# Moving four weight conversions and two splits behind the split of x, at the end of a first layer

## The chip, the cores and the metric

The kernel runs on one core of a Trainium2 chip. The metric is the device time of one launch in microseconds (us). Before the change three runs gave 817.26, 816.15 and 817.18 us, a median of 817.18 us.

Five engines take part, each with its own list of instructions that it works through strictly in the written order: PE (TensorE, matmuls), DVE (VectorE), ACT (ScalarE), POOL (GpSimd) and SP (SyncE, which here only issues DMA transfers). They wait for each other by semaphores.

## The reference

Clustered attention for 2 batches of 8 heads (768 positions, head size 64), then two feed-forward parts on the 1536 x 512 result x:

```
attn = softmax(where(same cluster, q @ k.T / 8, -1e9)) @ v     # per batch and head
a = x @ w1 ;  b = x @ w2                                        # 512 -> 1024  (the first layer)
h = ((a * b) @ w3) @ w_out                                      # 1024 -> 1024 -> 512
g = h2 @ w_in ; g = max(g, 0) + alpha * min(g, 0) ; g @ w_out2  # 512 -> 2048 -> 512
```

The weights arrive as 64-bit floats, all else is 32-bit; products are formed from a high and a low part of each factor.

## The kernel before, in words

**High and low parts.** Each factor of a matmul is held as two tiles in a reduced 32-bit format, a high part (a cast) and a low part (the difference). `mm3` (L243 to L246) forms one product with three matmuls: high x high, high x low, low x high.

**Weights.** They arrive as 64-bit words. For one tile of 128 x 512 weights the kernel does a *conversion* in two halves (`w_step`, L190): the first half loads the raw words of the conversion three places later (`w_load`, L132, a DMA on SP into one of **four** raw buffers `wr`), unpacks on ACT (L176, into `wu`) and joins the bits on DVE with three instructions (L181, L182, L185, into `wt`, two buffers). The second half casts on ACT (L226) and subtracts on POOL (L227). L182 is the last reader of a raw buffer on DVE, so a load on SP into a raw buffer waits for L182 of the conversion four places earlier.

**Reloads.** The high and low parts of the first layer's weights are stored to DRAM (`kept`, L148) when batch 0 uses them and are loaded again for batch 1 (L200, tile `wh`, one of five buffers). Batch 0 and batch 1 both go through the first layer in blocks of 128 outputs; a block takes two weight tiles, one for w1 (`l1a`) and one for w2 (`l1b`).

**One list sets the order of weights.** `seq` (L71 to L118) holds, in order: the first layer's 16 conversions (numbers 0 to 15), the conversions of four tiles of w_out (16 to 19, tiles `wo0`, `wo1`), the reloads of block 0 for batch 1 (20 and 21), two more conversions of w_out (22 and 23), the reloads of block 1 (24 and 25), two conversions (26 and 27), and so on. Numbers in names of tiles such as `wt17`, `wr22` and `wh20` are places in this list. `w_goal(n)` (L232) advances it by one half of a conversion if it has not passed n; `w_ready(key)` (L239) advances it until the wanted weights are there. Nothing in the list overtakes anything else, and what the list asks of SP is issued by SP in that order.

**The end of batch 0's first layer.** The attention loop (L729) interleaves attention with blocks 0 to 5 of the first layer of batch 0. Behind the loop, L807 runs what is left: blocks 6 and 7, in eight steps of 12 matmuls (l1a and l1b for each half of 384 positions, `a` = 0 and 1). After each step it calls `w_goal` up to conversion 23 (L808) and, while there is something ready, splits one finished product tile into high and low (`p_split`, L793: casts L799 on ACT, subtractions L800 on DVE, into `ph` and `pl`). The products themselves are `pr` (L594 on DVE, reading the PSUM result of l1b and a copy `asb` of l1a that ACT makes in L590).

**The split of x.** Then `x_split(1, p, a)` (L565) makes the high and low part of x for batch 1: eight casts on ACT (L570), four subtractions on DVE for a = 0 and four on POOL for a = 1 (L572), all into `xs`. `xs` for batch 1 lies in the buffer that `xs` for batch 0 held, so the first cast waits for the last matmul of batch 0's first layer. Behind it come the splits of products still open, then the first layer of batch 1 (L820), whose first matmul reads `wh20` and `xs`.

Of the kernel before, what the change touches and what calls it, by code (L numbers as in the profile page):

```python
# [28 lines left out]
def kernel(  # L29
# [41 lines left out]
    seq, at, keep, need = [], {}, {}, {}  # L71
# [118 lines left out]
    def w_step(force=False):  # L190

        n = st["step"]
        if n == NSEQ:
            return False
        kind, key, src = seq[n]
        if kind == "k":
            if not w_room():
                assert not force, key
                return False
            nc.sync.dma_start(out=f32(whl_tile(n)), in_=kept[src])  # L200
            st["step"] += 1
            return True
        m = ordinal[n]
        if not st["half"]:
            w_load(m + 3)
            while stores and ordinal[stores[0]] <= m - 2:
                w_store()
            w_u(m)
            w_conv(n)
            w_u(m + 1)  # L210
            st["half"] = 1
            return True
        if key[0] == "wo":
            if key[2] not in WO:
                return False
            hi, lo = WO[key[2]]
        else:
            if not w_room():
                assert not force, key
                return False  # L220
            t = whl_tile(n)
            hi, lo = his[key]
            if key[0] in ("l1", "w45", "e"):
                whole[n] = t
                stores.append(n)
        nc.scalar.copy(out=hi, in_=tts[n])  # L226
        nc.gpsimd.tensor_tensor(out=lo, in0=tts.pop(n), in1=f32(hi), op=ALU.subtract)  # L227
        st["half"] = 0
        st["step"] += 1
        return True  # L230

    def w_goal(n):  # L232

        while st["step"] <= min(n, NSEQ - 1):
            k = seq[st["step"]][0] == "k"
            if not w_step() or not k:
                return

    def w_ready(key):  # L239
        while st["step"] <= at[key]:  # L240
            w_step(True)
# [17 lines left out]
    def j_load(b, g, c):  # L259
        nc.sync.dma_start(out=j_raw(b, g)[:, c], in_=qka[b, g, c])  # L260
# [322 lines left out]
    def l1(b, f, a, alloc):  # L583

        if b not in PR:
            PR[b] = cp.tile([P, 8 * S], F32, tag="pr", name=f"pr{b}").rearrange("p (f s) -> p f s", f=8)
        t = alloc(f"l1a{b}{f}{a}")
        l1_mm(t[:, 0:HS], b, f, 0, a)
        q = wp.tile([P, HS], F32, tag="asb", name=f"asb{b}{f}{a}")
        nc.scalar.copy(out=q, in_=t[:, 0:HS])  # L590
        yield
        t = alloc(f"l1b{b}{f}{a}")
        l1_mm(t[:, 0:HS], b, f, 1, a)
        nc.vector.tensor_tensor(out=PR[b][:, f, a * HS : a * HS + HS], in0=t[:, 0:HS], in1=q, op=ALU.mult)  # L594
        yield


    with tc.manual_schedule():
# [45 lines left out]
        def l1_steps(b, f, ahead):  # L644
            for a in range(2):
                if a == 0:
                    w_ready(("l1", b, f, 1))
                for _ in l1(b, f, a, alloc_f):
                    w_goal(ahead)
                    yield f  # L650
# [10 lines left out]
        def fill_steps():  # L661

            yield from j01
            jm = cp.tile([P, 8 * S], F32, tag="wox", name="jm1")
            PR[0] = cp.tile([P, 8 * S], F32, tag="pr", name="pr0").rearrange("p (f s) -> p f s", f=8)
            sn = PR[0][:, 5:7].rearrange("p f s -> p (f s)")
            jmem[1, 0] = jm, jm[:, 3072 : 4608], jm[:, 5376 : 6144]
            jmem[1, 1] = jm, sn, PR[0][:, 7]
            for c in range(3):
                j_load(1, 0, c)  # L670
                yield
            j10, j11 = job(1, 0, alloc_f), job(1, 1, alloc_f)
            for k in range(5):
                next(j10)
                yield
            j_load(1, 1, 0)
            next(j10)
            yield
            for k in range(6):
                if k < 2:  # L680
                    j_load(1, 1, k + 1)
                next(j11)
                yield
            for _ in j10:
                yield
            for _ in j11:
                yield
            for _ in range(4):
                w_goal(1)
                yield  # L690
            while len(xdone) < 4:
                yield
            for f in range(8):
                yield from l1_steps(0, f, at["l1", 0, f, 0] + 3)


        cur = [alloc_s]
# [24 lines left out]

        xdone, fill_at = [], [0]
        fill = fill_steps()

        LT = 4
# [66 lines left out]
        def p_split(b, f, a):  # L793
            if (b, a) not in PH:
                for d, n in ((PH, "ph"), (PL, "pl")):
                    d[b, a] = big(f"{n}{a}", f"{n}{b}{a}").bitcast(F32R).rearrange("p (f s) -> p f s", f=8)
            s = slice(a * HS, a * HS + HS)
            ph, pl = PH[b, a][:, f], PL[b, a][:, f]
            nc.scalar.copy(out=ph, in_=PR[b][:, f, s])  # L799
            nc.vector.tensor_tensor(out=pl, in0=PR[b][:, f, s], in1=f32(ph), op=ALU.subtract)  # L800
# [4 lines left out]
        WO["wc"] = xp.tile([P, 2, 8, 512], F32R, tag="wc", name="wc")  # L805
        nsp = 0
        for f in fill:  # L807
            w_goal(at["wo", 0, 5, 0])  # L808
            if f is not None and nsp < f:
                p_split(0, nsp, 0), p_split(0, nsp, 1)  # L810
                nsp += 1
        for a in range(2):
# [140 lines left out]
```

## Time and profile before

| | us |
|---|---|
| median of three runs | 817.18 |
| the profiled execution | 814.83 |
| its span, first to last instruction | 812.7 |
| PE busy in the span | 760.2 (94%) |
| DVE busy | 525.1 (65%) |
| ACT busy | 452.1 (56%) |
| POOL busy | 303.1 (37%) |

The span is 2.13 us shorter than the profiled execution's own time. PE's 94% is an average: the attention stage (until about 334 us) has many short waits, and the stages behind it few. The rows below are of the stretch around 352 us, where batch 0's first layer ends and batch 1's begins.

### The profile page before, as it was taken

To read this page: it belongs to the slowest core of one execution; us is meant where nothing else is said; L and a number is where in the kernel's file an instruction comes from. 1 tells how busy PE (TensorE), PEld (TensorE's weight loads), DVE (VectorE), ACT (ScalarE), POOL (GpSimd) and SP (SyncE) were. 2 spreads that over 40 slices of the span, in tenths; PEclk is the share of its full clock that TensorE was granted. 3 is DMA by queue.
4 is the path that set the end of the run, shared out by engine and by line. 5 is a ranking of instruction groups with operands and counts; after the bars stand their busy time and mean duration, and the time that the engine had idled before them with its cause. 6 is when DMAs were issued, how large, how long until landed. Compare 5 with 4: busy or idle time off the path is not lost.

```text
span 812.7 us, 12622 instructions
## 1 busy us (share of the span) xinstructions
PE 760.2 (94%) x4497; PEld 699.8 (86%) x4497; DVE 525.1 (65%) x884; ACT 452.1 (56%) x980; POOL 303.1 (37%) x286
## 2 busy tenths in 40 slices
PE   5889899869999999969999999999999999999998
PEld 2678888769999998959999999998989878999996
DVE  3786899988888888885545599434456763322223
ACT  5799888877777787553223345324444453323232
POOL 0586778887676755433212343101112220000000
PEclk9899999999999999979999999999999999999999
DMA  7565343535464525755534588115665738333332
GB/s 243 179 173 159 85 97 83 133 93 162 130 179 127 165 77 157 233 181 181 181 130 158 173 276 289 64 40 194 192 204 182 219 135 280 122 121 127 128 130 78
DMA packets 38862, 127.27 MB, mean 157 GB/s; under 512 B 5168, under 2 KB 5296, under 8 KB 38800
## 3 DMA queue, kind: packets, MB, share of 16 engines
q1 hardware_dynamic: 38800, 126.46, 50.0%
q8 instruction: 36, 0.59, 0.3%
q14 instruction: 26, 0.21, 0.1%
HBM read 84.08 MB, written 28.31 MB: 138 GB/s over the span
## 4 chain that ended last, share of the span: by engine, by line
PE 65%; DVE 14%; ACT 5%; issue 4%; POOL 2%; DMA 1%; SPq 0%; POOLq 0%; ACTq 0%; DVEq 0%
PE l L246 7%; PE l L244 7%; PE l L245 7%; PE acc L245 5%; PE acc L246 5%; PE acc L244 5%; PE t L510 3%; DVE pl L520 3%; PE l1a L245 2%; PE l1a L244 2%; PE l1a L246 2%; PE l1b L245 2%; PE l1b L246 2%; PE l1b L244 2%; PE lc L245 2%
## 5 line engine op out<-in xcount | busy, mean ns | idle before, releaser
L227 POOL TENSOR_TENSOR wh<-wt,wh 128x512 fp32r<-128x512 f32 x64 | 86.3, 1348 | 232.2 <-ACT wh L226 160.3
L520 DVE TENSOR_TENSOR pl<-t,ph 128x384 fp32r<-128x384 f32 x192 | 97.5, 549 | 27.0 <-ACT ph L519 26.4
L867 DVE SCALAR_TENSOR_TENSOR gr<-gr,alp 128x384 f32<-128x384 f32 x64 | 41.6, 650 | 107.4 <-ACT gr L866 107.4
L510 PE MATMUL t<-cst,p 128*128 128x128 f32 x576 | 83.9, 282 | 22.3 <-DVE pl L520 22.2
L519 ACT CAST ph<-t 128x384 fp32r<-128x384 f32 x192 | 83.3, 484 | 30.1 <-PE t L510 28.6
L495 POOL TENSOR_SCALAR p<-p,su 128x768 f32<-128x768 f32 x96 | 91.9, 963 | 15.4 <-DVE su L492 13.2
L477 DVE TENSOR_REDUCE nm<-s 128x1 f32<-128x768 f32 x96 | 91.0, 948 | 3.2 <-PE s L470 3.2
L510 PEld LDWEIGHTS t<-cst,p 128*128 128x128 f32 x576 | 65.0, 143 | 30.9 <-issue 18.7
L484 ACT ACTIVATE p<-s,nm 128x768 f32<-128x768 f32 x96 | 88.2, 918 | 1.8 <-DVE nm L477 1.8
L469 PE MATMUL s<-st 128*128 128x384 f32 x192 | 75.1, 391 | 3.5 <-ACT p L484 3.5
L865 ACT ACTIVATE gr<-l 128x384 f32<-128x384 f32 x64 | 31.2, 487 | 80.6 <-PE l L246 80.6
L531 PE MATMUL o<-ph,vs 128*128 128x256 f32 x288 | 75.9, 291 | 0.0
L246 PE MATMUL acc<-wh,g 128*128 128x512 f32 x192 | 75.3, 392 | 0.0
L244 PE MATMUL acc<-wh,g 128*128 128x512 f32 x192 | 74.8, 390 | 0.6 <-ACT os L891 0.6
L245 PE MATMUL acc<-wh,g 128*128 128x512 f32 x192 | 75.3, 392 | 0.0
L532 PE MATMUL o<-pl,vs 128*128 128x256 f32 x288 | 73.8, 285 | 0.0
L182 DVE SCALAR_TENSOR_TENSOR wt<-wr,wt 128x512 uint32<-128x512 uint32 x72 | 70.5, 980 | 2.5
L470 PE MATMUL s<-st 80*128 80x384 f32 x192 | 67.5, 352 | 1.5 <-DMA st<-mk 1.5
L870 ACT CAST g<-gr 128x384 fp32r<-128x384 f32 x64 | 32.8, 513 | 59.5 <-DVE gr L867 59.5
L185 DVE SCALAR_TENSOR_TENSOR wt<-wu,wt 128x512 uint32<-128x512 uint32 x72 | 63.1, 876 | 2.5
L226 ACT CAST wh<-wt 128x512 fp32r<-128x512 f32 x64 | 39.8, 622 | 40.8 <-DVE wt L185 21.1
L544 POOL TENSOR_TENSOR xr<-xt 64x256 f32<-64x256 f32 x48 | 37.5, 782 | 64.6 <-ACT xt L543 57.7
(137 smaller groups left out, 1972.0 us busy)
## 6 DMA issues: line engine op xcount, KB each, us to landing
wh<-kept SPq DMA_DIRECT2D x58, 512.0 KB, 3.5
wr<-in_w_dram SPq DMA_DIRECT2D x48, 512.0 KB, 5.1
kept<-wh SPq DMA_DIRECT2D x48, 512.0 KB, 5.5
wr<-in_w3t_dram SPq DMA_DIRECT2D x16, 512.0 KB, 4.3
jm<-in_qka_dram SPq DMA_DIRECT2D x12, 512.0 KB, 5.6
hr<-in_qkh_dram SPq DMA_DIRECT2D x16, 384.0 KB, 3.4
st<-st SPq DMA_DIRECT2D x16, 384.0 KB, 3.7
st<-st SPq DMA_DIRECT2D x32, 192.0 KB, 2.7
```

What stands on the lines that cost most here:

```text
L227: nc.gpsimd.tensor_tensor(out=lo, in0=tts.pop(n), in1=f32(hi), op=ALU.subtract)
L244: nc.tensor.matmul(o, lhsT=whi, rhs=xhi, start=first, stop=False)
L245: nc.tensor.matmul(o, lhsT=whi, rhs=xlo, start=False, stop=False)
L246: nc.tensor.matmul(o, lhsT=wlo, rhs=xhi, start=False, stop=last)
L469: nc.tensor.matmul(t[:, a, 0:HS], lhsT=s[:, 0, q], rhs=s[:, 1, ks], start=True, stop=False)
L477: nc.vector.tensor_reduce(out=m, in_=scp[i][:, :, 0:HS], op=ALU.max, axis=AX.XY, negate=True)
L484: nc.scalar.activation(out=p.rearrange("p (a k) -> p a k", a=2), in_=scp.pop(i)[:, :, 0:HS], func=AF.Exp, bias=nmax.pop(i), scale=1.0, acc ...
L495: nc.gpsimd.tensor_scalar(out=pt[i], in0=pt[i], scalar1=sums[i // 2][:, i % 2 : i % 2 + 1], scalar2=1.0, op0=ALU.mult, op1=ALU.mult)
L510: nc.tensor.transpose(t[:, k], pt[i][:, kt * P : kt * P + P], ident)
L519: nc.scalar.copy(out=pth[g][:, 3 * a : 3 * a + 3, q], in_=t)
L520: nc.vector.tensor_tensor(out=ptl[g][:, 3 * a : 3 * a + 3, q], in0=t, in1=f32(pth[g][:, 3 * a : 3 * a + 3, q]), op=ALU.subtract)
L531: nc.tensor.matmul(ob[g], lhsT=w, rhs=pth[g][:, kt], start=(kt == 0), stop=False)
```

## The change

Three edits. In the attention loop's filler, block 7 no longer advances the weight list past its own weights (the number 3 becomes 0). In the loop over the remaining steps, the call that advanced the list by half a conversion per step is gone. And the splits of products inside that loop stop after six tiles, where they went on to seven.

```
@@ -691,7 +691,7 @@
             while len(xdone) < 4:
                 yield
             for f in range(8):
-                yield from l1_steps(0, f, at["l1", 0, f, 0] + 3)
+                yield from l1_steps(0, f, at["l1", 0, f, 0] + (3 if f < 7 else 0))
@@ -805,8 +805,7 @@
         WO["wc"] = xp.tile([P, 2, 8, 512], F32R, tag="wc", name="wc")
         nsp = 0
         for f in fill:
-            w_goal(at["wo", 0, 5, 0])
-            if f is not None and nsp < f:
+            if f is not None and nsp < min(f, 6):
                 p_split(0, nsp, 0), p_split(0, nsp, 1)
                 nsp += 1
```

What stands behind the loop is the same text in both kernels: the split of x, the splits of products still open (now tiles 6 and 7, before tile 7 alone), and the first layer of batch 1, which first calls `w_ready` for block 0's weights.

**DVE, blocks 6 and 7 of batch 0, before.** `pr0<-l1b060` is the product of block 6, half 0; `wt17` and `wt18` are conversions 17 and 18; `pl` are splits of products.

```order
L594 TENSOR_TENSOR pr0_506<-l1b060_4433,asb060_4421 128x384
L181 TENSOR_SCALAR wt17_4450<-wu17_4396 128x512
L182 SCALAR_TENSOR_TENSOR wt17_4450<-wr17_4305,wt17_4450 128x512
L185 SCALAR_TENSOR_TENSOR wt17_4450<-wu17_4396,wt17_4450 128x512
L800 TENSOR_TENSOR pl00_4426<-pr0_506,ph00_4425 128x384
L800 TENSOR_TENSOR pl01_4430<-pr0_506,ph01_4429 128x384
L800 TENSOR_TENSOR pl00_4426<-pr0_506,ph00_4425 128x384
L800 TENSOR_TENSOR pl01_4430<-pr0_506,ph01_4429 128x384
L594 TENSOR_TENSOR pr0_506<-l1b061_4468,asb061_4462 128x384
```

Behind these rows the product of block 6, half 1 is followed by conversion 18 in the same way, and so on: one conversion between two products.

**DVE, behind the last product of batch 0, now.** Ahead of these rows stand the product `pr0<-l1b071` and the first subtraction of the split of x; `xs1` is the split of x for batch 1, a = 0.

```order
L572 TENSOR_TENSOR xs1_4552<-xr5_2935,xs1_4552 128x384
L572 TENSOR_TENSOR xs1_4552<-xr6_3481,xs1_4552 128x384
L572 TENSOR_TENSOR xs1_4552<-xr7_3977,xs1_4552 128x384
L800 TENSOR_TENSOR pl00_4424<-pr0_506,ph00_4423 128x384
L800 TENSOR_TENSOR pl01_4428<-pr0_506,ph01_4427 128x384
L800 TENSOR_TENSOR pl00_4424<-pr0_506,ph00_4423 128x384
L800 TENSOR_TENSOR pl01_4428<-pr0_506,ph01_4427 128x384
L181 TENSOR_SCALAR wt17_4582<-wu17_4396 128x512
L182 SCALAR_TENSOR_TENSOR wt17_4582<-wr17_4305,wt17_4582 128x512
L185 SCALAR_TENSOR_TENSOR wt17_4582<-wu17_4396,wt17_4582 128x512
L181 TENSOR_SCALAR wt18_4592<-wu18_4586 128x512
L182 SCALAR_TENSOR_TENSOR wt18_4592<-wr18_4363,wt18_4592 128x512
```

Conversions 17, 18, 19 and 22 (twelve DVE instructions) moved from between the products to behind the split of x and the two last splits of products; 19 and 22 follow the rows shown, and then the first product of batch 1.

**SP, the loads and reloads around the same place, now; before, the same instructions stand in the same order.** `wr` are raw loads, `kept` a store, `wh20` and `wh21` the reloads that block 0 of batch 1 reads.

```order
L137 DMA wr22_4579<-in_wo_dram 128x1024
L148 DMA kept_73<-wh15_4386 128x1024
L137 DMA wr23_4590<-in_wo_dram 128x1024
L137 DMA wr26_4600<-in_wo_dram 128x1024
L200 DMA wh20_4610<-kept_73 128x1024
L200 DMA wh21_4612<-kept_73 128x1024
```

Nothing moved on SP; `wr23` goes into the raw buffer of conversion 17 and `wr26` into that of conversion 18. On POOL the subtractions (L227) of conversions 16 to 19 moved behind its four subtractions of the split of x, and on ACT their casts behind the eight casts of the split of x and the casts of the last two splits of products.

## Rows read from the trace of the kernel before

**Rows 1.** Waits of PE over the whole span: us in total, times, longest.
```profile
PE l1a L245 <- DVE xs L572: 4.0, 1, 4.0
PE l1a L244 <- DVE pl L800: 3.9, 1, 3.9
...
PE l L244 <- ACT gr L866: 1.2, 3, 0.5
```

**Rows 2.** Timeline of PE: start, length, instruction, [idle before <- releaser].
```profile
351.31 0.34 PE L246 MATMUL l1b<-xs,wh 128*128 128x384 f32 x1
355.57 0.69 PE L244 MATMUL l1a<-xs,wh 128*128 128x384 f32 x1 [3.93 <-DVE pl L800]
360.30 0.69 PE L245 MATMUL l1a<-xs,wh 128*128 128x384 f32 x1 [4.04 <-DVE xs L572]
360.78 0.52 PE L246 MATMUL l1a<-xs,wh 128*128 128x384 f32 x1
361.10 0.52 PE L244 MATMUL l1a<-xs,wh 128*128 128x384 f32 x1
...
364.36 0.34 PE L244 MATMUL l1b<-xs,wh 128*128 128x384 f32 x1
```

**Rows 3.** PE by stretch: us, PE busy (matmuls), granted clock, DMA share, GB/s.
```profile
352.00:356.00 4.00, 0.43 (x1) 0.73 0.57 198
356.00:360.00 4.00, 0.26 (x1) 0.50 0.34 112
360.00:364.00 4.00, 3.70 (x10) 0.50 0.74 282
364.00:368.00 4.00, 4.00 (x24) 0.99 0.00 0
```

**Rows 4.** Timeline of SP's queue and of ACT, 347 to 359 us.
```profile
347.20 0.33 SPq L137 DMA_DIRECT2D wr<-in_wo_dram  x1
347.58 0.90 SPq L200 DMA_DIRECT2D wh<-kept  x2
...
355.02 3.39 ACT L570 CAST xs<-xr 128x384 fp32r<-128x384 f32 x8
358.32 0.92 ACT L799 CAST ph<-pr 128x384 fp32r<-128x384 f32 x2
```

**Rows 5.** Timeline of DVE, 346 to 364 us.
```profile
346.43 0.69 DVE L182 SCALAR_TENSOR_TENSOR wt<-wr,wt 128x512 uint32<-128x512 uint32 x1
347.16 0.69 DVE L185 SCALAR_TENSOR_TENSOR wt<-wu,wt 128x512 uint32<-128x512 uint32 x1
347.77 1.02 DVE L800 TENSOR_TENSOR pl<-pr,ph 128x384 fp32r<-128x384 f32 x2
...
358.90 4.36 DVE L572 TENSOR_TENSOR xs<-xr,xs 128x384 fp32r<-128x384 f32 x4
```

**Rows 6.** Waits of SP's queue, 330 to 395 us; reloads in that stretch, issue to landing.
```profile
SPq L137 <- DVE wt L182: 47.3, 11, 9.4
...
DMA to landing us min/median/max: 3.1/4.9/6.0
```

**Rows 7.** Reloads issued 347.5 to 347.9 and 358.0 to 358.3 us: size, us to landing.
```profile
wh<-kept SPq DMA_DIRECT2D x1, 512.0 KB, 4.5
...
wh<-kept SPq DMA_DIRECT2D x1, 512.0 KB, 4.7
```

**Rows 8.** Timeline of POOL, 353 to 363 us.
```profile
353.81 1.34 POOL L227 TENSOR_TENSOR wo<-wt,wo 128x512 fp32r<-128x512 f32 x1 [3.87 <-ACT wo L226]
357.25 5.12 POOL L572 TENSOR_TENSOR xs<-xr,xs 128x384 fp32r<-128x384 f32 x4 [2.10 <-ACT xs L570]
```

**Rows 9.** DVE's L800, L181, L182: ns shortest/median/longest, 330 to 372 us.
```profile
L800 DVE TENSOR_TENSOR pl<-pr,ph x16: 545/551/1408, 338.6 to 363.6; 128x384 fp32r<-128x384 f32 x16
L181 DVE TENSOR_SCALAR wt<-wu x8: 409/414/774, 329.7 to 371.4; 128x512 uint32<-128x512 uint32 x8
L182 DVE SCALAR_TENSOR_TENSOR wt<-wr,wt x8: 691/693/1734, 330.1 to 371.8; 128x512 uint32<-128x512 uint32 x8
```

More of the change, by code (lines that the diff above doesn't have):

```diff
@@ L693, in fill_steps @@
             for f in range(8):
-                yield from l1_steps(0, f, at["l1", 0, f, 0] + 3)
+                yield from l1_steps(0, f, at["l1", 0, f, 0] + (3 if f < 7 else 0))
         cur = [alloc_s]
@@ L807 @@
         for f in fill:
-            w_goal(at["wo", 0, 5, 0])
-            if f is not None and nsp < f:
+            if f is not None and nsp < min(f, 6):
                 p_split(0, nsp, 0), p_split(0, nsp, 1)
```

## The prediction

> **What bounds the kernel now.** I read PE's waits first. Behind the attention stage PE has three waits in one place, the change from batch 0 to batch 1 in the first layer (4.0 and 3.9 us), and then next to none to the end of the span: the largest later line is 1.2 us in three waits [rows 1]. So from the first layer of batch 1 on, PE is the bound, and whatever delays or advances PE at this place moves the end by as much.
>
> The timeline of PE shows the place [rows 2]. The last matmul of batch 0 starts at 351.31 and ends at 351.65. The first of batch 1 starts at 355.57, the second at 360.30, and the next tile, l1b, at 364.36. The reader should see two things: two long holes, and matmuls 0.32 us apart (360.78 to 361.10), for which PE's granted clock was 0.50, that is 1.2 of 2.4 GHz, after it had stood nearly idle [rows 3]. The first 12 matmuls thus end 12.7 us after batch 0 did.
>
> What ended the two holes? The first matmul needs the reloaded weights `wh20` and the first cast of the split of x. `wh20` was issued at 347.58 and took 4.5 us, so it lay there at 352.1 [rows 4, 7]. ACT's casts of x began only at 355.02 [rows 4]; that ended the first hole (the row names a subtraction L800 on DVE, but the matmul follows the first cast by half a microsecond). The second hole ended with DVE's first subtraction of x, begun at 358.90 [rows 5]. DVE and ACT were late because a conversion stood between the products and the splits. The weights were early, and only just: 3 us.
>
> **The change part by part.**
>
> *What it takes away.* Conversions 17, 18, 19 and 22 leave DVE's, ACT's and POOL's lists ahead of the split of x, as does one split of products. DVE's part of one conversion is 0.41 + 0.69 + 0.69, 1.85 us from start to start of what follows [rows 5, 9]. Without them DVE follows PE: the last product starts at about 351.75 and ends at 352.3, since it waits for the last matmul (351.65). ACT's first cast of x waits for the same matmul, because the new tile lies in the old one's buffer: 351.7. So x's first high part would be there at 352.2 and its first low part at 352.9. By the split of x alone PE would start 3.4 us sooner and not wait a second time.
>
> *What it moves, and who stands behind it.* SP's list is unchanged, and in it the reloads `wh20` and `wh21` stand behind the raw loads `wr23` and `wr26`. A raw load waits for the L182 of the conversion whose buffer it takes; such waits are most of SP's waiting, 47.3 us in eleven [rows 6]. The traced load at 347.20 is `wr26`: it left 0.08 us behind the end of conversion 18's L182 (346.43 + 0.69), and `wh20` 0.38 us behind it [rows 4, 5]. The change puts conversion 18 behind the split of x and the last two splits of products on DVE. So `wh20`, which lay ready at 352.1, is now issued only when DVE has come through all that. This is the wait that takes the place of the one removed, and it is worked out along DVE:
>
> 1. Split of x. POOL's first subtraction followed ACT's first cast by 2.23 us (355.02 to 357.25) [rows 4, 8], so now POOL begins at 353.9. Until then DVE runs at the 0.5 us a piece that a pair takes alone (1.02 for two) [rows 5], three of its four subtractions; the fourth ends at 354.4.
> 2. Splits of tiles 6 and 7. ACT's eight casts take 3.39, until 355.1, and its next cast 0.5 [rows 4]: the first of four `pl` starts at 355.6. POOL is in its subtractions until 353.9 + 5.12 = 359.0 [rows 8]. Beside POOL, DVE's four subtractions of x took 4.36 us [rows 5]; alone two `pl` took 1.02. Bounds for the four: 2.0 alone and 4 x 1.408 = 5.6 at the longest seen [rows 9]. I take 4.4, the row with POOL in the same work: 360.0. (At the lower bound ACT's casts, two in 0.92, hold them to 357.5.)
> 3. Conversion 17: 1.85 alone; POOL's L227 of conversion 16, 1.34 long [rows 8], runs from 359.0 to 360.3, so I add 0.3 for the overlap: 362.15. Bounds 1.85, and 0.77 + 1.73 + 0.69 = 3.2 with the longest L181 and L182 [rows 9].
> 4. Conversion 18 up to L182: 0.42 + 0.69 and the gap, 1.15: 363.3. Upper bound 0.77 + 1.73 = 2.5.
> 5. SP: 0.08 + 0.38: `wh20` is issued at 363.75. Two reloads in the same neighbourhood, each right behind a raw load, landed after 4.5 and 4.7 us [rows 7]; all of the stretch lie between 3.1 and 6.0 [rows 6]. With 4.7: 368.45.
> 6. PE starts then, everything else being ready, on the lower clock as in the traced start [rows 3]: 12 matmuls at 0.32, 3.8 us, so l1b starts at 372.25. Bounds 2.0 (at full clock 24 matmuls fill a stretch of 4.0 [rows 3]) and 4.1, what eleven took before with waits in them.
>
> On the Trainium skill, SBUF — State Buffer, section "Who interferes with whom": a DVE operation with two operands in SBUF and a GpSimd operation that reads SBUF exclude each other, the second to come standing still until the first is done. Here the shortest `pl` is 545 ns and the longest 1408, which a lock with an operation of POOL in the way would give, so the trace does not speak against it [rows 9]. Applied to every `pl` and L182 beside POOL, it is the long case below.
>
> The Trainium skill, DMA: Bandwidth & Descriptors, section "Anatomy of one DMA", fits a transfer as 2.0 us plus its bytes at 436 GB/s (for descriptors made by software). For 512 KB this is an estimate of 3.2 us against the 4.5 and 4.7 measured; by it the sum would be 1.5 us smaller. The measurement stands.
>
> *The sum.* l1b starts at 372.25 instead of 364.36: 7.9 us later. The later conversions on DVE end at about 368, ahead of the first product of batch 1, and the reloads of block 1, behind conversion 22, have until 372.25 + 3 x 2.0 (12 matmuls at full clock), about 378.2; both lie beside PE's work. If that cover failed, it would show as a PE wait at block 1. Nothing later gives time back, since PE hardly waits later [rows 1]. The profiled execution, 814.83 with its span of 812.7, would become 822.7; it lay 2.35 below the median of the three runs, 817.18, and that becomes 825.1. I forecast 825.
>
> At the lower bounds together (357.5, then 1.85, 1.15, 0.46, a landing in 3.1, 2.0 on PE) l1b starts at 366.05, 1.7 us late: 818.9. At the upper bounds of the DVE steps (355.6 + 5.6 + 3.2 + 2.5 = 366.9), a landing in 6.0 and 4.1 on PE, 377.5: 13.1 us late, 830.3.
>
> **The rivals.**
>
> *Faster: the split of x decides alone.* If `wh20` is not held back (the raw load ahead of it gets its buffer at the old time), PE starts at 352.2, and l1b follows at 355 to 356.7 by the two spacings: 7.7 to 9.4 us gained, 807.8 to 809.5. For it: both holes of the trace are those of the split of x [rows 2]. Against it: SP issues in its written order, and the row at 347.20 leaves 0.08 us behind the very instruction that moves. It decides if `wh20` lands before 352.2.
>
> *No change.* Between the two: `wh20` lands about when PE now goes on, near 360.3 and less the 0.5 that the waits inside cost. That asks for conversion 18's L182 at about 355.5, when ACT has just ended its casts of x and two splits and a conversion still lie ahead. Only a DVE list other than the one shown would give it.
>
> *The lock everywhere.* Every `pl` takes 1.408, and L182 1.73 beside POOL's L227: four `pl` until 361.2, conversion 17 until 364.4, the next L182 at 366.5, `wh20` at 371.65 and l1b at 375.5, 11.1 us late, 828.3. The page of the skill named above would make this the rule. Against it: the four subtractions of x took 4.36 beside POOL, not 5.6 [rows 5], and POOL has only four of its own left to put in the way.
>
> **How the numbers follow.** The forecast (5 to 10 us slower) gets 0.76. The lock everywhere (over 10) gets 0.08. A smaller loss (1.7 to 5 us: short landing, DVE hardly hindered) gets 0.07. Faster gets 0.06, no change 0.03. A measurement of this kernel can tell 0.2%, 1.6 us, from no change. So slower is 0.91, within 0.2% is 0.03, faster 0.06. The range leaves out the faster and unchanged cases and the far ends of the slower ones: 821 to 829.
>
> **What would show it.** In the changed profile, ACT's casts of x begin near 351.7 and DVE's first subtraction of x near 352.3; that step is right even if the time is not. SP's wait for DVE's L182 at `wr26` ends near 363.4. PE has one hole of about 16.8 us instead of 3.9 and 4.0, ended by a DMA into `wh`, then 12 matmuls at clock 0.50. DVE's `pl` of the last two tiles are the widest term. I am wrong if PE's first matmul of batch 1 follows the cast of x by less than a microsecond, or if reloads are issued before 355.

## The result and the profile after

The changed kernel took 824.78 us (median of four runs, 822.12 to 825.47) against 816.66 for the kernel before (four runs, 816.03 to 817.26): a ratio of 1.0097, 95% interval 1.0074 to 1.0119, or 8.1 us slower. Forecast were 7.9 slower and 825. That the medians meet the forecast so closely is partly luck: the interval spans 6.0 to 9.7 us, and the stretch that the change touches grew by 9.3, as shown below.

The profiled executions differ by more, 825.47 to 814.83, and the reason has to be cleared away before anything is compared. In the profile after, batch 0's first layer ends at 353.40, in the one before at 351.65 [rows 2]. The change did not make that difference: the very first matmul of the first layer, far ahead of anything that moved, starts at 183.35 before and at 185.09 after, so 1.74 of the 1.75 us are there already. Over the twelve profiles of this study, one for each kernel, the end of batch 0's first layer lies between 350.51 and 356.14. From here on times are counted from that end, called E, in each profile. A second mark, the first matmul that joins w3 and w_out (tile `lc`), closes the stretch, three blocks later.

PE's longest waits in the profile after (us in total, times, longest):

```profile
PE t L510 <- DVE pl L520: 21.8, 21, 4.2
PE l1a L244 <- DMA wh<-kept: 17.6, 1, 17.6
...
PE l1a L244 <- DVE pr L594: 0.7, 1, 0.7
```

The two waits of before [rows 1] are gone; one wait of 17.6 for a reload stands there. Timeline of PE after, and then its granted clock by stretch (us, PE busy, clock, DMA share, GB/s):

```profile
353.06 0.34 PE L246 MATMUL l1b<-xs,wh 128*128 128x384 f32 x1
370.95 0.66 PE L244 MATMUL l1a<-xs,wh 128*128 128x384 f32 x1 [17.56 <-DMA wh<-kept]
371.41 0.52 PE L245 MATMUL l1a<-xs,wh 128*128 128x384 f32 x1
...
374.93 0.52 PE L244 MATMUL l1b<-xs,wh 128*128 128x384 f32 x1
...
377.48 0.33 PE L244 MATMUL l1a<-xs,wh 128*128 128x384 f32 x1
...
398.28 0.39 PE L244 MATMUL lc<-wo,wh 128*128 128x512 f32 x1
```

```profile
362.00:366.00 4.00, 0.00 (x0) 0.50 0.38 131
366.00:370.00 4.00, 0.00 (x0) 0.50 0.93 310
370.00:374.00 4.00, 3.04 (x10) 0.50 0.96 368
374.00:378.00 4.00, 4.00 (x20) 0.76 0.62 240
```

From E to `l1b` were 364.36 - 351.65 = 12.71 before and are 374.93 - 353.40 = 21.53 now, 8.8 more; the lower clock lasts three matmuls into `l1b`, and to `lc` it is 398.28 - 353.40 = 44.88 against 35.60 (before, `lc` starts at 387.25), 9.3 more. From `lc` to the end of the span it is 823.7 - 398.28 = 425.4 now and 812.7 - 387.25 = 425.4 before: nothing was given back and nothing lost later.

Timelines of DVE and of SP's queue after, 353 to 366 us:

```profile
353.50 0.56 DVE L594 TENSOR_TENSOR pr<-l1b,asb 128x384 f32<-128x384 f32 x1 [2.74 <-PE l1b L246]
353.98 1.96 DVE L572 TENSOR_TENSOR xs<-xr,xs 128x384 fp32r<-128x384 f32 x4
357.28 4.96 DVE L800 TENSOR_TENSOR pl<-pr,ph 128x384 fp32r<-128x384 f32 x4 [1.34 <-ACT ph L799]
362.16 0.41 DVE L181 TENSOR_SCALAR wt<-wu 128x512 uint32<-128x512 uint32 x1
...
364.40 0.69 DVE L182 SCALAR_TENSOR_TENSOR wt<-wr,wt 128x512 uint32<-128x512 uint32 x1
```

```profile
363.37 2.13 SPq L137 DMA_DIRECT2D wr<-in_wo_dram  x2
365.55 0.90 SPq L200 DMA_DIRECT2D wh<-kept  x2
```

This is the chain of the forecast, link by link: the split of x starts with the end of batch 0 (its four subtractions on DVE now take 1.96 us where they took 4.36 [rows 5]), then four `pl`, then conversion 17, then conversion 18's L182, which ends at 365.09; 0.08 later SP issues the raw load that stood ahead, and 0.46 later the reload. In the kernel before, the same reload was issued 4.1 us ahead of batch 0's end. SP's longest single wait for L182 was 24.6 us; it was 9.4 [rows 6].

### The profile page after: what moved, and what is told of

It is laid out like the page before. It is cut to its first block, busy times and chain, and to the rows that moved or that the text cites. A ratio compares the mean times of both kernels' runs of the same rounds, so it can differ in the third digit from the quotient of the medians.

```text
span 823.7 us, 12629 instructions
## 1 busy us (share of the span) xinstructions
PE 762.4 (93%) x4497; PEld 703.7 (85%) x4497; DVE 525.6 (64%) x884; ACT 451.9 (55%) x980; POOL 302.6 (37%) x286
## 4 chain that ended last, share of the span: by engine, by line
PE 67%; DVE 10%; ACT 6%; issue 4%; POOL 2%; DMA 1%; SPq 0%; POOLq 0%; ACTq 0%; DVEq 0%
PE l L246 7%; PE l L244 7%; PE l L245 7%; PE acc L245 5%; PE acc L246 5%; PE acc L244 5%; PE t L510 4%; PE l1a L244 3%; DVE pl L520 3%; PE l1a L246 3%; PE l1a L245 3%; PE l1b L244 2%; PE l1b L246 2%; PE l1b L245 2%; PE lc L245 2%
## 5 line engine op out<-in xcount | busy, mean ns | idle before, releaser
L227 POOL TENSOR_TENSOR wh<-wt,wh 128x512 fp32r<-128x512 f32 x64 | 86.2, 1347 | 231.7 <-ACT wh L226 145.0
L495 POOL TENSOR_SCALAR p<-p,su 128x768 f32<-128x768 f32 x96 | 91.6, 959 | 18.5 <-DVE su L492 16.4
L510 PEld LDWEIGHTS t<-cst,p 128*128 128x128 f32 x576 | 65.4, 144 | 30.6 <-issue 18.8
L182 DVE SCALAR_TENSOR_TENSOR wt<-wr,wt 128x512 uint32<-128x512 uint32 x72 | 70.5, 980 | 2.5
L185 DVE SCALAR_TENSOR_TENSOR wt<-wu,wt 128x512 uint32<-128x512 uint32 x72 | 65.2, 906 | 2.5
L244 PE MATMUL l1a<-xs,wh 128*128 128x384 f32 x128 | 44.8, 350 | 18.3 <-DMA wh<-kept 17.6
```

Source lines behind the costliest of these rows:

```text
L244: nc.tensor.matmul(o, lhsT=whi, rhs=xhi, start=first, stop=False)
L495: nc.gpsimd.tensor_scalar(out=pt[i], in0=pt[i], scalar1=sums[i // 2][:, i % 2 : i % 2 + 1], scalar2=1.0, op0=ALU.mult, op1=ALU.mult)
L510: nc.tensor.transpose(t[:, k], pt[i][:, kt * P : kt * P + P], ident)
```

## The experiments

All figures in one table: the median, its ratio to runs of the kernel before on the same chip, and from one profile each, E to `lc`. In e3 and w2 inserted lines move the line numbers of the rows below by 3 (L203 is L200 of the other kernels), in e8, w4 and b5 by 1.

| kernel | us | ratio (95% interval) | E to `lc`, us |
|---|---|---|---|
| before | 816.66 | | 35.60 |
| after | 824.78 | 1.0097 (1.0074 to 1.0119) | 44.88 |
| e1_split_only | 814.73 | 0.9985 (0.9963 to 1.0007) | 34.42 |
| e2_conv_only | 822.67 | 1.0078 (1.0049 to 1.0107) | 44.05 |
| e3_reload_first | 823.22 | 1.0078 (1.0054 to 1.0102) | 40.56 |
| e5_conv_ahead | 823.89 | 1.0101 (1.0065 to 1.0137) | 42.35 |
| e6_pe_kept_busy | 823.25 | 1.0084 (1.0069 to 1.0098) | 42.46 |
| w1_two_early | 817.04 | 1.0010 (0.9994 to 1.0025) | 36.61 |
| w2_two_early_spread | 817.95 | 1.0015 (1.0004 to 1.0026) | 36.67 |
| e8_loads_on_act | 814.12 | 0.9977 (0.9959 to 0.9994) | 34.06 |
| w4_two_early_loads_on_act | 808.15 | 0.9896 (0.9877 to 0.9915) | 27.40 |
| b5_before_loads_on_act | 817.52 | 1.0013 (1.0000 to 1.0025) | 35.51 |

From `lc` to the end of the span the profiles take 425.4 to 426.3 us, but 427.6 in e6 and 427.7 in w4: about 2 us of what these two gain in the stretch do not reach the end of their profiles. In w4, 0.9 of it are waits at `lc`; the rest is not explained.

**Each half of the change alone.** e1 is the kernel before with `min(f, 6)` and nothing else; e2 is the kernel after with `nsp < f` again.

> The kernel before with one edit alone: split of products 6 goes behind the split of x, the conversions stay where they were. Theory (the reloaded weights decide the loss, the split of x decided before): the reloads are issued as before and lie ready 3 us early, and DVE's first subtraction of x comes 1.9 us sooner (the two pl that took 1.86 us ahead of the last product), so PE's second matmul of batch 1 comes about 57 us... that is, 6.7 us after batch 0's last matmul ended instead of 8.65; the time is 1 to 2 us below before, about 815. Rival (moving splits behind x makes batch 1 late, since the first product of batch 1 stands behind them on DVE): the time is 1 us or more above before.

> The kernel after, with seven splits of products ahead of the split of x again; only the conversions are moved. Theory: the reload waits behind two pl fewer on DVE, which took 1.24 us each beside POOL (4.96 for four), so wh20 is issued about 2.5 us earlier after the end of batch 0 than after's 12.15, and PE starts 15 us after that end instead of 17.55; the time is about 2.5 us below after, near 822.3. Rival (the moved splits cause the loss): the time falls back to that of before, near 816.7.

PE's waits in e1, then in e2:

```profile
359.25 0.44 PE L244 MATMUL l1a<-xs,wh 128*128 128x384 f32 x1 [3.12 <-ACT xs L570]
362.71 0.69 PE L245 MATMUL l1a<-xs,wh 128*128 128x384 f32 x1 [3.02 <-DVE xs L572]
```

```profile
368.11 0.66 PE L244 MATMUL l1a<-xs,wh 128*128 128x384 f32 x1 [16.24 <-DVE wt L182]
```

SP's queue in e2:

```profile
362.98 0.90 SPq L200 DMA_DIRECT2D wh<-kept  x2
```

Moving a split alone shortens both old holes, by 0.8 and 1.0 us (the second matmul comes 362.71 - 356.14 = 6.6 us after E, as expected); 1.2 us less to `lc`, which the runs cannot tell from no change. Moving the conversions alone makes nearly all of the loss. (The row of e2 names an L182 on DVE, which the matmul does not read; the reload landed 5.0 us behind its issue, 0.13 ahead of the matmul.) The reload's hole is 1.3 us shorter than in after; expected were 2.5: with two `pl` fewer, conversion 17 ran beside POOL's subtractions instead (its L181 and L182 took 1.21 and 1.63 there). Of the 1.3 only 0.8 are left at `lc`, since 18 matmuls ran on the lower clock where 15 did in after. So the median, 822.67, meets the expected 822.3, but the step behind it was half as large. The loss belongs to the conversions.

**Is it the reload?** e3 puts the reloads of block 0 ahead of conversions 17 to 19 in the list, and leaves the other engines' order as after has it:

```
     for g in range(4):
         conv("wo", g, 0)
+        if g == 0:
+            back("l1", 1, 0, 0), back("l1", 1, 0, 1)
...
+            if f:
                 back("l1", 1, f, 0), back("l1", 1, f, 1)
...
+        w_ready(("wo", 0, 3, 0))
         for n, f in enumerate(BLOCKS):
```

> The kernel after, with the two reloads of block 0 put ahead of conversions 17, 18 and 19 in the list of weights; DVE, ACT and POOL keep after's order, only SP's order changes. Theory: the reloads no longer wait for a conversion; PE starts about 0.6 us after batch 0 ends, is then held up again where its sixth tile needs the PSUM of the first (whose copy on ACT stands behind the cast of conversion 19, 16 us after the end), and the whole comes out 4 us below before, 808 to 815. Rival (the pile of conversions on DVE, ACT and POOL behind the split of x costs the time, with or without the reload): 822 or more.

PE's waits in e3, then conversion 22's L182 (here L185) on DVE, then SP's queue:

```profile
353.90 0.45 PE L247 MATMUL l1a<-xs,wh 128*128 128x384 f32 x1 [0.60 <-ACT xs L573]
375.70 0.69 PE L247 MATMUL l1a<-xs,wh 128*128 128x384 f32 x1 [12.67 <-DMA wh<-kept]
```

```profile
369.88 0.69 DVE L185 SCALAR_TENSOR_TENSOR wt<-wr,wt 128x512 uint32<-128x512 uint32 x1
```

```profile
370.65 0.33 SPq L140 DMA_DIRECT2D wr<-in_w3t_dram  x1
371.07 0.86 SPq L203 DMA_DIRECT2D wh<-kept  x2
```

The time fell where the rival had put it, and yet the profile does not show the rival. PE starts 0.6 us after E, as the theory says, runs four tiles and then stands for 12.67 us: for the reloads of block 1, which SP issues right behind a raw load that waited for conversion 22's L182. The theory was too narrow. It is not one reload that is tied to one conversion; in the list the reloads of each later block stand behind raw loads too, and the next ones caught PE a block later. Only 4.3 us of the stretch came back, and of the median only 1.6 (823.22, where 808 to 815 were expected); why the median shows less than the one profile is not known.

**Two conversions early.** w1 lets block 6 advance the list by four halves, so 17 and 18 stay ahead of the split of x; w2 also moves block 0's reloads ahead of conversion 19 and advances the list twice per step in block 0 of batch 1.

```
         for f in fill:
+            if f == 6:
+                w_goal(at["wo", 0, 5, 0])
             if f is not None and nsp < min(f, 6):
```

> The kernel after, but block 6 still advances the list of weights by four halves, so conversions 17 and 18 stay ahead of the split of x, and 19 and 22 move behind it. Theory: conversion 18's L182 ends well before batch 0 does, the reloads lie ready, and the split of x starts with the end of batch 0: PE's first matmul of batch 1 about 0.6 us and its second 1.2 us after that end, its second tile after about 3.3 us instead of 12.7 in before: about 9.4 us below before, near 807.3. Rival (conversions 19 and 22 and the four pl behind the split of x hold PE at its sixth tile through PSUM): half of that is lost, near 812.

> As w1_two_early, with the reloads put ahead of conversion 19 in the list, so that conversion 19's second half and what follows it need not precede block 0 of batch 1, and with two halves instead of one per step in that block. Theory: as w1_two_early within 1 us, near 807, since PE was not held by the conversions there. Rival (PE is held by them in w1_two_early): 1 to 4 us below w1_two_early.

Both missed by 10 us, and again in the same way. PE in w1, then conversion 22's L182 on DVE, then SP's queue:

```profile
352.26 0.41 PE L244 MATMUL l1a<-xs,wh 128*128 128x384 f32 x1 [0.72 <-DVE pr L594]
369.54 0.69 PE L244 MATMUL l1a<-xs,wh 128*128 128x384 f32 x1 [8.23 <-DMA wh<-kept]
```

```profile
362.68 0.69 DVE L182 SCALAR_TENSOR_TENSOR wt<-wr,wt 128x512 uint32<-128x512 uint32 x1
```

```profile
363.44 0.33 SPq L137 DMA_DIRECT2D wr<-in_w3t_dram  x1
363.83 0.90 SPq L200 DMA_DIRECT2D wh<-kept  x2
```

The expected start is there (0.7 us after E), the two old holes are gone, and one of 8.23 stands at block 1, behind conversion 22; in w2 it is one of 8.7. The kernel before spent 8.0 in its two holes.

**Take the raw loads out of SP's list.** e8 is after, w4 is w1, b5 is before, each with this edit and nothing else. On ACT such a load stands behind the cast of the conversion before, which waits for later DVE work than the load does.

```
-            nc.sync.dma_start(out=r..., in_=seq[n][2].bitcast(U32))
+            q = nc.scalar if 20 <= st["load"] < 40 else nc.sync
+            q.dma_start(out=r..., in_=seq[n][2].bitcast(U32))
```

> The kernel after, with the raw loads of conversions 22 to 41 or so (20 loads) issued by ACT instead of SP, so that on SP nothing but stores stands ahead of the reloads; the order on DVE, POOL and PE is after's. e3_reload_first moved the hole from block 0 to block 1, whose reloads still stood behind a raw load. Theory (SP's order ties each reload to a conversion, and behind that DVE's list of conversions is the next bound): no wait of PE for a reload is left in the first layer of batch 1; PE starts 0.6 us after batch 0 ends and is then paced by DVE, whose conversions 16 to 31 end about 35 us after that end, about as late as in before: 813 to 816. Rival (the pile on DVE, ACT and POOL alone makes the loss): 822 or more, as e3_reload_first.

> w1_two_early (conversions 17 and 18 ahead of the split of x) with the same 20 raw loads on ACT. Theory: no wait for a reload, and DVE has two conversions, 4 to 5 us, less to do behind the split of x than in e8_loads_on_act: the first matmul that joins w3 and w_out comes about 30 us after the end of batch 0 instead of 35.5 in before: 810 to 812. Rival (issuing loads on ACT delays its casts, or another wait takes the place again): 816 or more.

> The kernel before with the same 20 raw loads on ACT and nothing else. Theory (in before the reloads lay ready 3 us early and the split of x decided, so taking the raw loads off SP frees nothing that PE waits for): 816 to 818, no change, with both holes of before (3.9 and 4.0 us) still there. Rival (loads on ACT are themselves what made w4_two_early_loads_on_act 8 us faster): 812 or less.

PE's waits in e8, in w4 and in b5, 345 to 450 us (us in total, times, longest):

```profile
PE l1b L245 <- ACT asb L591: 5.5, 1, 5.5
PE l1a L245 <- ACT xs L571: 0.6, 1, 0.6
```

```profile
PE lc L247 <- POOL wh L228: 0.9, 2, 0.6
PE l1a L245 <- ACT xs L571: 0.6, 1, 0.6
PE lc L245 <- ACT wh L227: 0.6, 1, 0.6
```

```profile
PE l1a L246 <- DVE xs L573: 4.0, 1, 4.0
PE l1a L245 <- ACT xs L571: 3.9, 1, 3.9
```

In e8, the first `l1b` of batch 1 on PE, then a conversion's cast and the first `asb` on ACT:

```profile
355.09 0.33 PE L245 MATMUL l1b<-xs,wh 128*128 128x384 f32 x1
```

```profile
368.12 0.62 ACT L227 CAST wo<-wt 128x512 fp32r<-128x512 f32 x1 [1.51 <-DVE wt L186]
368.65 0.47 ACT L591 COPY asb<-l1a 128x384 f32<-128x384 f32 x1
```

This settles it. e8 has after's order on DVE, POOL and PE and is 0.23% faster than before (interval 0.06 to 0.41) where after is 0.97% slower: without the raw loads ahead of the reloads the loss is gone. No wait for a reload is left, and `l1b` starts 3.2 us after E, 9.5 sooner than before. But only 1.5 of the 9.5 are left at `lc`. The next bound is the one named, the pile of conversions, seen as a wait of 5.5 us for ACT's copy `asb` of the first tile, which the sixth tile needs out of PSUM and which stands behind the casts of the conversions. w4 has two conversions less in that pile and waits 2.1 us in all; it is the fastest kernel here, 1.04% below before and 2 us below the range expected. There `lc` started 27.4 us after E, with the first of its two weight tiles; the second was through DVE 30.0 after E, the time that the expectation took for the start. b5 shows that the loads on ACT give nothing by themselves: before's two holes are both there. The gain needs both, the split of x free of conversions and the reloads free of raw loads.

**The order behind the split of x.** e5 puts the conversions ahead of the last two splits of products:

```
+        w_ready(("l1", 1, 0, 1))
         while nsp < 8:
             p_split(0, nsp, 0), p_split(0, nsp, 1)
```

> The kernel after, with the conversions that stand behind the last two splits of products put ahead of them (split of x, conversions 16 to 19, then splits 6 and 7). Theory: the four pl (4.96 us) no longer stand ahead of conversion 18's L182, but conversion 18 needs the wt buffer of conversion 16, which POOL frees only behind its four subtractions of x and one L227 (6.8 + 1.5 us after the end of batch 0), so L182 ends about 9.5 us after that end instead of 11.7: 2.2 us below after, near 822.6. Rival (only DVE's queue counts): all 5 us come back, near 819.8.

DVE in e5, conversion 18, and PE's wait:

```profile
360.33 1.47 DVE L181 TENSOR_SCALAR wt<-wu 128x512 uint32<-128x512 uint32 x1 [2.11 <-POOL wo L227]
361.83 0.69 DVE L182 SCALAR_TENSOR_TENSOR wt<-wr,wt 128x512 uint32<-128x512 uint32 x1
```

```profile
367.58 0.66 PE L244 MATMUL l1a<-xs,wh 128*128 128x384 f32 x1 [15.86 <-ACT ph L799]
```

The wait for POOL is the one expected (2.11 us, then 1.47 for an L181 that takes 0.41 alone), the gain smaller: L182 ends 10.8 us after E instead of 11.7 (9.5 was expected), and the reload is issued 0.9 sooner. The stretch is 2.5 us shorter all the same, near the 2.2 expected, but partly by luck: the reload landed in 4.5 us instead of 5.3, so that PE waits 15.86 instead of 17.56 (the matmul starts 0.1 behind this landing and reads nothing of the L799 that the row names), and 9 matmuls ran on the lower clock instead of 15. The median lies 0.9 below after's, too little for these runs to tell. The rival's 5 us are excluded: its 819.8 would be 0.34% above before, below the interval.

**The clock.** e6 puts 96 matmuls that nothing reads into the hole:

```
+        idle = alloc_c("idle")
+        hi = his["l1", 0, 7, 1][0]
+        for k in range(96):
+            nc.tensor.matmul(idle[:, 0:HS], lhsT=hi[:, 0:P], rhs=PH[0, 0][:, 0], start=True, stop=True)
```

> The kernel after, with 96 extra matmuls of 128x384 on PE between the last matmul of batch 0 and the first of batch 1; nothing reads what they compute, nothing else changes. At 0.173 us each they take 16.6 us, a little less than the hole of 17.55. Theory (the loss is the hole, and on top of it the lower clock behind it): the hole is as long as before, but the first 15 matmuls of batch 1, 0.32 us apart in after, come at 0.173: 2.2 us below after from the end of batch 0 to the second l1a tile (24.08 in after, about 21.9 here). Rival (the granted clock costs nothing that other waits would not take): 24.1 here as well.

Stretches of e6 (us, PE busy, clock, DMA share, GB/s), and the first matmul of the first and of the second `l1a` tile:

```profile
366.00:370.00 4.00, 3.25 (x20) 1.00 0.98 390
370.00:374.00 4.00, 4.00 (x25) 1.00 0.91 330
```

```profile
369.52 0.41 PE L244 MATMUL l1a<-xs,wh 128*128 128x384 f32 x1 [0.75 <-DMA wh<-kept]
373.79 0.33 PE L244 MATMUL l1a<-xs,wh 128*128 128x384 f32 x1
```

The clock stayed at 1.00, 2.4 GHz, and from E (352.13) to the second `l1a` it took 21.66 where after took 24.08 (377.48 - 353.40). PE starts 0.16 sooner, still when the reload lands, so the lower clock costs 2.3 us there; expected were 2.2. The kernel before restarts on the lower clock too [rows 2, 3], so the clock is little of the difference between before and after.

## Why the prediction was right

By its own steps, each as time after E, forecast and measured:

| step | forecast | measured |
|---|---|---|
| DVE's first subtraction of x | 0.65 | 0.58 |
| first `pl` of the last two splits | 3.95 | 3.88 |
| four `pl` done | 8.35 | 8.84 |
| conversion 17 done | 10.5 | 10.55 |
| conversion 18's L182 done | 11.65 | 11.69 |
| `wh20` issued | 12.1 | 12.15 |
| PE's first matmul | 16.8 | 17.55 |
| `l1b` starts | 20.6 | 21.53 |

The mechanism was right: the wait for the split of x was removed and the reload's wait took its place. Up to the issue of `wh20` the sum is off by 0.05 us, partly by luck: the four `pl` took 4.96 and not 4.4, and conversion 17 took 1.79 and not 2.15. POOL's L227 ran beside the last `pl` (which ended at 362.24) and not beside the conversion:

```profile
360.25 1.57 POOL L227 TENSOR_TENSOR wo<-wt,wo 128x512 fp32r<-128x512 f32 x1
```

The term that was mis-sized is the landing: 5.3 us instead of 4.7. A likely reason is that the raw loads `wr23` and `wr26` were issued 1.8 us apart just ahead of it, where the last two raw loads ahead of the reloads whose landing I took were 5.2 apart. The other profiles fit: the landing took 5.0, 5.0 and 5.7 in e2, e6 and w1, where these loads were 1.8 apart, and 4.6, 4.6 and 4.5 in e1, e3 and e5, where they were 5.2, 2.8 and 5.7 apart; no run changed this alone. The rest is the clock: 12 matmuls took 3.98 and not 3.8, and three more ran slowly behind them.

*The rival "faster"* (the split of x alone decides) was refuted at its decision point: `wh20` left at E + 12.15. e8 is the kernel that it describes, after's order with nothing that holds the reloads: `l1b` does start 9.5 us sooner than before there (7.7 to 9.4 were promised), but the pile of conversions takes most of it back, and the time was 814.12 and not 807.8 to 809.5. With two conversions less in the pile, in w4, 8.2 us are left at `lc`. *No change* has no support. *The lock everywhere* was too dear: the `pl` beside POOL's subtractions took 1.24 on average, not 1.41, and both L182 their 0.69. Operations beside POOL did get longer, but where PE was not held by them: the L185 of conversions 18, 19 and 22 took 1.64 each and not 0.69.

One sentence of the prediction was less sure than it sounded: that the later conversions and the reloads of block 1 lie beside PE's work. They did in after, since PE came so late itself, although the conversions ended 18.8 us after E and not 16.4; e3 and w1 show that a PE that starts on time waits for these reloads 12.67 and 8.23 us. And one reading was wrong without weight: PE has two waits in that place, not three; the third, of 0.7, stands at 334.71, where the attention stage ends.

## What to carry to other kernels

A queue that issues in order ties together transfers that have nothing to do with each other: before moving compute, look at which DMA issue waits for it, and at what stands behind that issue. When a wait is taken away and the time does not fall, look for the same wait one step later, as with the reloads of block 1; the cure was to separate the two kinds of load, not to reorder them, and what it gave depended on the next bound. And compare two profiles by stage, from a mark ahead of the place to a mark behind it, when an untouched stage ahead scatters by several us.

## What the runs showed that was not expected

That 20 raw loads on ACT, at 0.33 to 0.38 us of its queue each, cost nothing that can be seen: b5's stretch is 35.51 against 35.60 (its times allow up to 0.25%, 2 us).

That in e8 and w4 conversions on DVE, packed without gaps, took 3.3 us a piece with one product between them and not 1.85 + 0.55, with an L182 of about 1.74 in each that ran beside POOL's L227. One such L182 in w4 (here L183):

```profile
371.44 1.74 DVE L183 SCALAR_TENSOR_TENSOR wt<-wr,wt 128x512 uint32<-128x512 uint32 x1
```

POOL's L227 (here L228) ran from 371.34 to 372.63 beside it. It took 1.29 there as it did before, so it is DVE that loses, about 1 us per conversion.

And one of the four runs of after took 822.12 with a mean granted clock of 0.981 where the others had 0.971 or 0.972; the 2.5 us are about the size of the clock's share in e6, but no trace of that run exists, so its cause stays open.
